# Loading the sorting network from SyncE ahead of q, dropping three trial instructions, and a newly searched instruction order in a fused attention and feed-forward kernel

## The chip, the cores and the metric

The kernel runs on one core of a Trainium2 chip. A core has TensorE (PE in the profile), VectorE (DVE), ScalarE (ACT), GpSimd (POOL) and SyncE (SP), each with its own stream of instructions, and 16 DMA engines that all of its transfers share. The metric is the device time of one execution in microseconds (us). A comparison gives the median of several runs.

## What is computed

Input are q, k, v of shape (4 batches, 8 heads, 768 positions, 64 channels), a sorting network `sort_net` of one 8x8 matrix for each of the 32 heads, and the two weights of a feed-forward part, `w_in` (512x2048) and `w_out` (2048x512), all float32.

```python
P = sort_net
for _ in range(5):
    P = exp(P - max(P, axis=-1))
    P = P / (sum(P, axis=-1) + 1e-09)
    P = P / (sum(P, axis=-2) + 1e-09)
k_sorted = einsum('bhij,bhjcd->bhicd', P, k in 8 blocks of 96 positions)
v_sorted = einsum('bhij,bhjcd->bhicd', P, v in 8 blocks of 96 positions)
attn = softmax(q_block @ k_sorted_block.T / 8)      # 96x96, block by block
x = (attn @ v_sorted_block), heads side by side      # 3072 rows x 512
out = relu(x @ w_in) ** 2 @ w_out                    # 3072 x 512
```

So five rounds of exponentials and row and column sums on the small matrices (Sinkhorn) come before everything else: no block of k or v can be mixed before they are done.

## The kernel before, in words

**Stages.** Work on TensorE goes in this order. First a start: `p_sb` (the 32 small matrices) is loaded, five Sinkhorn rounds alternate between ScalarE (the exponential, L465) and VectorE (sums, reciprocals and products, `sink_norm`, L409 to L413); meanwhile TensorE runs filler matmuls on a tile of ones (`fill`, L438) and transposes q of batch 0 (L578). Then `p_spread` (L489) brings P into the form from which the mixing weights `w_all` are built. Then comes batch 0, first halves, by a hand-written list, `FIRST`. Each entry is a letter for a step and a digit for the pair of heads: K and V mix k and v with P (L628), S makes scores (L699), T transposes v (L748), A multiplies by the values (L890), X transposes the result into `xT` (L943), F begins a feed-forward product (L970). An upper-case letter has its result copied out of PSUM by ScalarE, a lower-case one by VectorE; a prime, together with the kind of the step, says which of two pools of PSUM tiles it takes.

**The rest** is one stream of matmuls. The feed-forward part is cut into eight units of 384 rows: 64 matmuls "up" (L1012, four for each of 16 column tiles), a Relu on ScalarE (L1020), a square on VectorE (L1023), and three tiles of 16 matmuls "down" (L1042; the last tile of all is L1070). Steps of the attention of the batches to come are put between them: `s_sort2` (L664) mixes the second halves of batch 0, `s_nat` (L784) mixes k or v of the later batches, S and A as above. For v of batches 1 to 3 the mixed tile `vn` is written to DRAM (`v_way`, L808) and read back in another layout (`vblk`, L814) for A; k, q and most results are turned by DMA transposes (L839, L866, L925). All of these transfers and the outputs (L991) are issued by SyncE, in one queue, in one order.

**Loads.** SyncE first issues float32 q of heads 0 to 3 of batch 0 into spare space of `xT` (`q32`, two transfers, L270), and ScalarE casts them to bf16 (L473). ScalarE itself issues one transfer, that of `p_sb` (L265). GpSimd issues all other loads (L324): q of heads 4 to 7, k and v of batch 0, `w_in` and `w_out` in four parts each, then v, k and q of batch 1, and later batches 2 and 3 when a small copy has seen that a batch is done (L1159).

**Who decides the order.** `Plan` is a list scheduler that runs while the kernel is built. Every step is given an engine, a cost and its dependencies, and so is every transfer, as an operation on a pretended engine "DMA" or "WAY" with an assumed duration. TensorE has two lists, attention and feed-forward, each kept in its own order; an attention step goes ahead of a feed-forward step when it is ready and its due number is not above the count of feed-forward steps already placed. The due numbers are the table `DUES`, by batch and step: N and V are `s_nat` of k and v, Z the DMA transposes, L the loads of a batch, Q the first steps of batch 1, W the weights `w_t` that `s_nat` uses. The emitted instructions carry no times, only this order and the waits on data. Where the plan leaves TensorE idle before the feed-forward part, it puts in filler matmuls that last as long as the planned gap.

**Trial instructions.** Beside the real work there are three that compute nothing that is used: two float32 matmuls (L448) in `warm`, one exponential with an accumulated sum (L452) behind the first Sinkhorn exponential, and one reciprocal from PSUM (L456) in the third round. They have a VectorE memset (L443) as their input.

Of the kernel before, what the change touches and what calls it, by code (L numbers as in the profile page):

```python
# [8 lines left out]
FP32 = mybir.dt.float32  # L9
BF16 = mybir.dt.bfloat16  # L10
AF = mybir.ActivationFunctionType
# [10 lines left out]
    (0, "K"): (-242.5, -237.0, -449.5, -391.0),  # L22
    (0, "S"): (-214.5, -217.0, -359.5, -370.5),
    (0, "T"): (-167.5, -226.5, -373.0, -268.5),
    (0, "A"): (-159.0, -195.0, -306.0, -99.0),
    (0, "X"): (-124.0, -130.5, -290.5, -94.5),
    (0, "W"): (-245.5,),
    (1, "V"): (-115.0, -110.5),
    (1, "Q"): (-94.0,),
    (1, "N"): (None, -50.5),  # L30
    (1, "Z"): (None, None, 33.5, 34.0),
    (1, "S"): (-53.0, -3.0, 38.5, 51.0),
    (1, "A"): (-45.5, 3.5, 45.5, 51.0),
    (1, "X"): (43.5, 24.5, 56.0, 53.5),
    (2, "L"): (60.0,),
    (2, "N"): (66.5, 69.5),
    (2, "V"): (63.5, 79.5),
    (2, "Z"): (77.5, 81.5, 85.5, 81.5),
    (2, "S"): (80.0, 84.0, 102.5, 97.0),
    (2, "A"): (82.0, 86.0, 102.5, 98.0),  # L40
    (2, "X"): (90.5, 118.0, 111.0, 114.0),
    (3, "L"): (123.0,),
    (3, "N"): (132.0, 141.0),
    (3, "V"): (128.0, 138.5),
    (3, "Z"): (133.5, 133.5, 149.5, 143.0),
    (3, "S"): (147.0, 153.0, 161.0, 158.0),
    (3, "A"): (147.0, 154.5, 162.0, 158.5),
    (3, "X"): (156.5, 161.5, 195.0, 182.0),
# [4 lines left out]
FIRST = ("K0' v0 K1 v1 S0 t0' S1 t1' A0 K2' V2 A1 K3 S2 t2' v3' S3 x1' A2 T3' x0 A3 X2' F1 F0 "  # L53
         "F4 F3 F7 F6 X3")
# [130 lines left out]
def kernel(  # L185
# [10 lines left out]
    nc = tc.nc  # L196

    B, H, S, D = q.shape
# [31 lines left out]
    plan = Plan()  # L230
# [34 lines left out]
    nc.scalar.dma_start(out=p_sb, in_=sort_net.rearrange("b h i j -> (b h) i j"))  # L265
# [53 lines left out]
    landed = {}  # L319

    def dma(key, mb, dst_src, deps=(), long=True, rate=0.23):
        def issue(e):
            dst, src = dst_src()
            nc.gpsimd.dma_start(out=dst, in_=src)  # L324
        op = plan.add("POOL", 0.75, issue, deps)
        landed[key] = plan.add("DMA", mb / (0.39 if key[0] == 0 else 0.43 if long else rate), lambda e: None, [op, landed.get("last")])
        landed["last"] = landed[key]
# [25 lines left out]
    first = plan.add("DMA", 3.95, lambda e: None)  # L353
# [88 lines left out]
    t32 = xT[:, 3, 2 * S:].bitcast(FP32)  # L442
    nc.vector.memset(t32[:, 0:136], 1.0)  # L443

    def warm(e):
        fill(2.4, 0)
        for n in range(2):
            nc.tensor.matmul(out=p2[1][:, 0, 8 * n:8 * n + 8], lhsT=t32[:, 0:128],  # L448
                             rhs=t32[:, 128:136], start=True, stop=True)

    def try_exp(e):
        nc.scalar.activation(out=t32[:, 144:152], in_=t32[:, 128:136], func=AF.Exp,  # L452
                             accum_out=t32[:, 152:153])

    def try_rec(e):
        nc.vector.reciprocal(out=t32[:, 160:168], in_=p2[1][:, 0, 8:16])  # L456
# [7 lines left out]
    for it in range(5):  # L464
# [3 lines left out]
        if it == 0:  # L468
            plan.add("ACT", 0.3, try_exp, [step])
        if it < 2:  # L470
            def cast(e, g=it):
                alloc_qkv(0)
                nc.scalar.copy(out=qkv[0][0][:, 2 * g:2 * g + 2, :], in_=q32[g])  # L473

            casts.append(plan.add("ACT", 0.83, cast, [step, plan.add(
                "WAY", 3.5 + 0.9 * it, lambda e: None, tail=3.5 + 0.9 * it)]))
# [4 lines left out]
        if it == 2:  # L481
            plan.add("DVE", 0.0, try_rec, [step])
# [737 lines left out]
```

## Time and profile before

| | us |
|---|---|
| three runs | 218.44, 219.02, 220.64 (median 219.02) |
| the profiled execution's own time | 218.59 |
| its span, first to last instruction of the program | 216.8 |
| TensorE busy | 209.8 |
| ScalarE, VectorE busy | 121.4, 109.9 |
| GpSimd busy | 28.4 |
| mean granted TensorE clock | 0.998 of full speed |

A profile line of a group gives the line of the kernel, the engine, the operation, the tile written and the tiles read; `x16` is the number of instructions. "idle before, releaser" is how long the engine had nothing to run ahead of these and what ended it. The chain that ended last is followed back from the last instruction. Since matmuls are pipelined and their ends are modelled, the distance from the start of one group to the start of the next is the better measure of what a group costs on TensorE: 4 matmuls up are 0.65 us, 4 down 0.865 us, 16 of `s_nat` 0.31 us, 16 of S 0.45 us, 8 of A 0.25 us.

### The profile page before, as it was taken

To read this page: it belongs to the slowest core of one execution; us is meant where nothing else is said; L and a number is where in the kernel's file an instruction comes from. 1 tells how busy PE (TensorE), PEld (TensorE's weight loads), DVE (VectorE), ACT (ScalarE), POOL (GpSimd) and SP (SyncE) were. 2 spreads that over 40 slices of the span, in tenths; PEclk is the share of its full clock that TensorE was granted. 3 is DMA by queue.
4 is the path that set the end of the run, shared out by engine and by line. 5 is a ranking of instruction groups with operands and counts; after the bars stand their busy time and mean duration, and the time that the engine had idled before them with its cause. 6 is when DMAs were issued, how large, how long until landed. Compare 5 with 4: busy or idle time off the path is not lost.

```text
span 216.8 us, 5097 instructions
## 1 busy us (share of the span) xinstructions
PE 209.8 (97%) x2040; PEld 116.1 (54%) x2040; DVE 109.9 (51%) x300; ACT 121.4 (56%) x252; POOL 28.4 (13%) x53
## 2 busy tenths in 40 slices
PE   8898999799999999999999999999999999999994
PEld 3466765346655555445665455445655565456542
DVE  4778576345894447643895045517675154015300
ACT  5777985227783268436774177328865375147421
POOL 7994320000000700000000330000000000000000
PEclk9999999999999999999999999999999999999999
DMA  6999999999968799939852599599884310120012
GB/s 183 194 204 207 206 208 209 194 173 292 225 125 76 136 211 228 188 102 194 187 153 64 121 192 215 105 208 229 98 209 115 91 48 3 48 97 0 0 51 97
DMA packets 47864, 31.92 MB, mean 147 GB/s; under 512 B 27296, under 2 KB 42912, under 8 KB 47840
## 3 DMA queue, kind: packets, MB, share of 16 engines
q1 hardware_dynamic: 35568, 18.34, 37.8%
q0 software_dynamic: 12224, 13.24, 37.8%
q8 instruction: 16, 0.26, 0.5%
q14 instruction: 8, 0.07, 0.1%
q10 hardware_dynamic: 48, 0.01, 0.0%
HBM read 29.70 MB, written 8.72 MB: 177 GB/s over the span
## 4 chain that ended last, share of the span: by engine, by line
PE 81%; DMA 14%; POOL 3%; issue 1%; ACT 0%; POOLq 0%
PE op L1042 36%; PE hp L1012 34%; DMA vb<-in_v_dram 9%; DMA w_in_bf<-in_moe_w_in_dram 5%; PE p L890 3%; PE p L699 3%; PE p L784 2%; PE op L1070 2%; POOL vb L324 1%; POOL kb L324 1%; POOL qb L324 1%; PE qtp L578 0%; PE p L628 0%; PE xtp L943 0%; POOL ident masks.py:199 0%
## 5 line engine op out<-in xcount | busy, mean ns | idle before, releaser
L1012 PE MATMUL hp<-xT,w_in_bf 128*128 128x384 bf16 x506 | 88.1, 326 | 0.0
L1042 PE MATMUL op<-w_out_bf,h 128*128 128x512 bf16 x368 | 84.6, 379 | 0.0
L1020 ACT ACTIVATE h<-hp 128x384 bf16<-128x384 f32 x128 | 61.7, 495 | 17.8 <-PE hp L1012 14.7
L1023 DVE TENSOR_TENSOR h<-h 128x384 bf16<-128x384 bf16 x128 | 43.6, 354 | 44.2 <-ACT h L1020 43.8
L1012 PEld LDWEIGHTS <-w_in_bf 128*128 128x128 bf16 x506 | 47.3, 98 | 31.2 <-issue 0.7
L1042 PEld LDWEIGHTS <-h 128*128 128x128 bf16 x368 | 33.9, 98 | 38.3 <-issue 1.2
L248 ACT COPY ob<-op 128x512 f32<-128x512 f32 (+2 forms) x23 | 13.1, 568 | 48.7 <-PE op L1042 46.3
L728 ACT ACTIVATE et<-p 96x384 bf16<-96x384 f32 x48 | 19.7, 488 | 9.3 <-PE p L699 9.3
L901 DVE TENSOR_TENSOR ao<-p,rec 96x512 bf16<-96x512 f32 x32 | 22.0, 686 | 1.3 <-DVE rec L900 0.2
L890 PEld LDWEIGHTS <-et 96*128 96x128 bf16 x256 | 11.7, 97 | 5.2 <-issue 0.7
L250 DVE CAST vn<-p 128x768 bf16<-128x768 f32 x6 | 5.7, 958 | 15.1 <-PE p L784 10.7
L900 DVE RECIPROCAL rec<-p 96x8 f32<-96x8 f32 x32 | 6.4, 201 | 10.3 <-PE p L890 8.7
L1159 POOL COPY held<-xT 1x3 bf16<-1x3 bf16 (+1 forms) x2 | 0.4, 186 | 85.8 <-DMA xT<-ao 85.8
L248 ACT CAST vn<-p 128x768 bf16<-128x768 f32 x6 | 4.8, 800 | 9.1 <-PE p L784 9.1
L890 PE MATMUL p<-vblk,et 96*128 96x65 bf16 x192 | 9.6, 193 | 0.0
L438 PE MATMUL p<-ones 128*128 128x512 bf16 (+1 forms) x28 | 8.5, 433 | 1.1 <-DVE ones L274 1.1
L699 PEld LDWEIGHTS <-kvT 64*128 64x128 bf16 x256 | 6.2, 94 | 5.4 <-issue 3.1
L844 DVE COPY kvT<-kx 128x768 bf16<-128x768 bf16 x10 | 8.4, 847 | 0.0
L250 DVE CAST kn<-p 128x768 bf16<-128x768 f32 x5 | 4.8, 956 | 5.5 <-PE p L784 5.5
L324 POOL DMA_DIRECT2D kb<-in_k_dram x10 | 6.5, 646 | 4.1 <-DMA w_out_bf<-in_moe_w_out_dram 1.8
L324 POOL DMA_DIRECT2D vb<-in_v_dram x10 | 6.3, 630 | 3.0 <-DMA w_in_bf<-in_moe_w_in_dram 3.0
L324 POOL DMA_DIRECT2D qb<-in_q_dram x8 | 6.0, 750 | 2.7 <-DMA w_in_bf<-in_moe_w_in_dram 1.9
(88 smaller groups left out, 120.0 us busy)
## 6 DMA issues: line engine op xcount, KB each, us to landing
out_dram<-ob SPq DMA_DIRECT2D x23, 256.0 KB, 3.2
v_way<-vn SPq DMA_DIRECT2D x6, 396.0 KB, 5.3
vblk<-v_way SPq DMA_DIRECT2D x6, 396.0 KB, 4.1
vb<-in_v_dram POOLq DMA_DIRECT2D x6, 384.0 KB, 11.9
kb<-in_k_dram POOLq DMA_DIRECT2D x6, 384.0 KB, 10.4
qb<-in_q_dram POOLq DMA_DIRECT2D x6, 384.0 KB, 13.4
w_in_bf<-in_moe_w_in_dram POOLq DMA_DIRECT2D x4, 512.0 KB, 11.1
w_out_bf<-in_moe_w_out_dram POOLq DMA_DIRECT2D x4, 512.0 KB, 16.3
```

Source lines behind the costliest of these rows:

```text
L248: nc.scalar.copy(out=out, in_=in_)
L250: nc.vector.tensor_copy(out=out, in_=in_)
L324: nc.gpsimd.dma_start(out=dst, in_=src)
L438: nc.tensor.matmul(out=p2[slot][:, 0, 0:128 * r].rearrange("p (r x) -> p r x", r=r), lhsT=ones, rhs=ones[:, None, :].to_broadcast([128, r, ...
L699: nc.tensor.matmul(out=scp[:, h, BLK * n:BLK * (n + 1)], lhsT=u.ksT[64 * h:64 * (h + 1), HS * hf + BLK * n:HS * hf + BLK * n + 128], rhs=( ...
L728: nc.scalar.activation(out=et[:, h, 0:HS].rearrange("p (n c a) -> p n c a", c=C0, a=NA), in_=st["p"][0:96, h, 0:HS].rearrange("p (n a c) - ...
L890: nc.tensor.matmul(out=oup[:, h, 66 * n:66 * n + D + 1], lhsT=et_r[u.et[hf]][:, h, BLK * n:BLK * n + 128], rhs=(u.vs[:, NQ * hf + n, h, 0: ...
L901: nc.vector.tensor_tensor(out=u.ao[:, n0:n0 + NQ, :, :].rearrange("p n e d -> p e n d"), in0=ov[:, :, :, 0:D], in1=rec[:, :, :, None].to_b ...
L1012: nc.tensor.matmul(out=t["hp", nt][:, 0:HS], lhsT=w_in_bf[:, kc, 128 * nt:128 * (nt + 1)], rhs=xT[:, kc, t0:t0 + HS], start=(kc == 0), sto ...
L1020: nc.scalar.activation(out=t["h1", nt], in_=t["hp", nt][:, 0:HS], func=AF.Relu)
L1023: nc.vector.tensor_tensor(out=t["h2"][:, nt, :], in0=t["h1", nt], in1=t["h1", nt], op=ALU.mult)
L1042: nc.tensor.matmul(out=t["op", mt], lhsT=t["h2"][:, nt, 128 * mt:128 * (mt + 1)], rhs=w_out_bf[:, nt, :], start=(nt == 0), stop=(nt == NT ...
```

## The change

The load of `p_sb` is issued by SyncE as its first transfer, so that ScalarE issues none and the two transfers of `q32` come behind it in SyncE's queue. The casts of `q32` on ScalarE move from behind the first and second exponential to behind the second and third. The three trial instructions and their memset are gone. In the plan, loads of batch 0 are given a higher rate and every load a lag after its transfer, and the first landing moves from 3.95 to 4.15. With these assumptions `DUES` and `FIRST` are replaced.

```diff
-    (0, "K"): (-242.5, -237.0, -449.5, -391.0),
+    (0, "K"): (-265.0, -237.0, -495.0, -419.0),
...
-    (1, "V"): (-115.0, -110.5),
-    (1, "Q"): (-94.0,),
+    (1, "V"): (-117.0, -62.5),
+    (1, "Q"): (-58.5,),
...
-    (1, "S"): (-53.0, -3.0, 38.5, 51.0),
+    (1, "S"): (-45.5, -5.0, 5.0, 50.0),
...
-FIRST = ("K0' v0 K1 v1 S0 t0' S1 t1' A0 K2' V2 A1 K3 S2 t2' v3' S3 x1' A2 T3' x0 A3 X2' F1 F0 "
-         "F4 F3 F7 F6 X3")
+FIRST = ("K0' v0 K1 v1 S0 t0' S1 t1' A0 K2' V2 A1 K3 S2 t2 v3 S3 x1' A2 T3' x0' A3 X2' F0 F1 F3 "
+         "F4 F6 F7 X3")
...
-    nc.scalar.dma_start(out=p_sb, in_=sort_net.rearrange("b h i j -> (b h) i j"))
+    nc.sync.dma_start(out=p_sb, in_=sort_net.rearrange("b h i j -> (b h) i j"))
...
-        landed[key] = plan.add("DMA", mb / (0.39 if key[0] == 0 else 0.43 if long else rate), lambda e: None, [op, landed.get("last")])
-        landed["last"] = landed[key]
+        landed["last"] = plan.add("DMA", mb / (0.43 if key[0] == 0 or long else rate), lambda e: None, [op, landed.get("last")])
+        lag = ((0.4 if key[1] == 0 else 1.7 if key[1:3] == (2, H - 2) else 0.9) if key[0] == 0
+               else 0.05 if key[0] in (2, 3) else 1.9)
+        landed[key] = plan.add("DMA", lag, lambda e: None, [landed["last"]], tail=lag)
...
-    first = plan.add("DMA", 3.95, lambda e: None)
+    first = plan.add("DMA", 4.15, lambda e: None)
...
-    t32 = xT[:, 3, 2 * S:].bitcast(FP32)
-    nc.vector.memset(t32[:, 0:136], 1.0)
-
     def warm(e):
         fill(2.4, 0)
-        for n in range(2):
-            nc.tensor.matmul(out=p2[1][:, 0, 8 * n:8 * n + 8], lhsT=t32[:, 0:128],
-                             rhs=t32[:, 128:136], start=True, stop=True)
-
-    def try_exp(e):
-        nc.scalar.activation(out=t32[:, 144:152], in_=t32[:, 128:136], func=AF.Exp,
-                             accum_out=t32[:, 152:153])
-
-    def try_rec(e):
-        nc.vector.reciprocal(out=t32[:, 160:168], in_=p2[1][:, 0, 8:16])
...
-        if it == 0:
-            plan.add("ACT", 0.3, try_exp, [step])
-        if it < 2:
-            def cast(e, g=it):
+        if it in (1, 2):
+            def cast(e, g=it - 1):
...
-                "WAY", 3.5 + 0.9 * it, lambda e: None, tail=3.5 + 0.9 * it)]))
+                "WAY", (4.3, 5.8)[it - 1], lambda e: None, tail=(4.3, 5.8)[it - 1])]))
...
-        if it == 2:
-            plan.add("DVE", 0.0, try_rec, [step])
```

The instruction streams that this gives differ as follows. **TensorE, start:** the two trial matmuls are gone; behind the ten first filler matmuls stand 12 transposes of q, 6 fillers, 36 transposes, 4 fillers, and from there the same run as before (12 transposes and 1, 1, 3 and 2 fillers between, then `p_spread`); there are 28 fillers in both. **TensorE, batch 0:** the groups of `FIRST` stand in the same order, only the pools differ and the F pieces are exchanged in pairs. **TensorE, unit 0:** ahead of the first `s_nat` of batch 1's v stand 28 matmuls down instead of 8, with the same 64 up, mixes, S and A ahead of them; between the first and the second `s_nat` of v stand 12 matmuls down, an A and a transpose (20 matmuls down before). **TensorE, later:** 8 matmuls up now stand ahead of the transposes of q of batch 1; the first A that reads `vblk` stands behind 36 matmuls up instead of 28; some S groups of 16 are split into two of 8 or joined, and single `s_nat` groups of batches 2 and 3 change places. **SyncE:** one output transfer goes ahead of the first `v_way` write (none before), one stands between the first and the second as before, and one behind the second instead of two; of the later transfers some change places by one or two. **GpSimd:** the same instructions in the same order.

More of the change, by code (lines that the diff above doesn't have):

```diff
@@ L21 @@
 DUES = {
-    (0, "K"): (-242.5, -237.0, -449.5, -391.0),
[L23 to L27, printed above, removed]
-    (1, "V"): (-115.0, -110.5),
-    (1, "Q"): (-94.0,),
-    (1, "N"): (None, -50.5),
-    (1, "Z"): (None, None, 33.5, 34.0),
-    (1, "S"): (-53.0, -3.0, 38.5, 51.0),
[L33 to L48, printed above, removed]
-}
-FIRST = ("K0' v0 K1 v1 S0 t0' S1 t1' A0 K2' V2 A1 K3 S2 t2' v3' S3 x1' A2 T3' x0 A3 X2' F1 F0 "
-         "F4 F3 F7 F6 X3")
+    (0, "K"): (-265.0, -237.0, -495.0, -419.0),
+    (0, "S"): (-232.5, -234.0, -349.0, -310.0),
+    (0, "T"): (-184.0, -236.0, -400.0, -291.5),
+    (0, "A"): (-135.0, -150.0, -300.0, -111.0),
+    (0, "X"): (-58.0, -109.0, -251.5, -80.5),
+    (0, "W"): (-267.0,),
+    (1, "V"): (-117.0, -62.5),
+    (1, "Q"): (-58.5,),
+    (1, "N"): (None, -31.0),
+    (1, "Z"): (None, None, 2.5, 48.5),
+    (1, "S"): (-45.5, -5.0, 5.0, 50.0),
+    (1, "A"): (-27.0, -4.5, 31.5, 51.5),
+    (1, "X"): (40.0, 23.5, 37.0, 53.5),
+    (2, "L"): (40.0,),
+    (2, "N"): (75.5, 79.0),
+    (2, "V"): (60.5, 82.5),
+    (2, "Z"): (81.0, 82.5, 94.0, 83.5),
+    (2, "S"): (86.0, 86.5, 96.0, 93.5),
+    (2, "A"): (86.0, 88.0, 99.0, 94.5),
+    (2, "X"): (97.5, 103.0, 103.0, 102.0),
+    (3, "L"): (109.0,),
+    (3, "N"): (111.5, 130.0),
+    (3, "V"): (112.5, 144.0),
+    (3, "Z"): (128.5, 139.0, 153.0, 149.0),
+    (3, "S"): (144.0, 153.0, 158.0, 153.5),
+    (3, "A"): (145.0, 153.5, 159.5, 154.5),
+    (3, "X"): (150.5, 170.0, 236.5, 211.5),
+}
+FIRST = ("K0' v0 K1 v1 S0 t0' S1 t1' A0 K2' V2 A1 K3 S2 t2 v3 S3 x1' A2 T3' x0' A3 X2' F0 F1 F3 "
+         "F4 F6 F7 X3")
 class Op:
```

## The prediction

> **What bounds the kernel now.** I read the page's busy times first, then its chain, then TensorE's waits, then the chain in order of time, and last ScalarE's and TensorE's timelines of the first 13 us.
>
> ```profile
> PE 209.8 (97%) x2040; PEld 116.1 (54%) x2040; DVE 109.9 (51%) x300; ACT 121.4 (56%) x252; POOL 28.4 (13%) x53
> ...
> PE 81%; DMA 14%; POOL 3%; issue 1%; ACT 0%; POOLq 0%
> ```
>
> TensorE is busy 97% of the span, and the chain is TensorE but for some DMA. So only two things can move the end: when the stream of matmuls starts, and where it stands still. TensorE's waits name the latter:
>
> ```profile
> PE p L784 <- DMA vb<-in_v_dram: 1.4, 1, 1.4
> PE p L438 <- DVE ones L274: 1.1, 1, 1.1
> PE qtp L578 <- ACT qb L473: 0.6, 1, 0.6
> PE p L890 <- ACT qz L248: 0.5, 1, 0.5
> ```
>
> One wait is in the steady part: `s_nat` waits 1.4 us for v of batch 1. The chain says when:
>
> ```profile
> 18.89 20.09 DMA vb<-in_v_dram
> 38.98 0.04 issue
> 39.03 0.39 PE p L784 x16
> 39.41 4.42 PE op L1042 x20
> ```
>
> v lands at 38.98, and 20 matmuls down stand right behind the step that waits for it. From 39.03 to 213.65 the chain is TensorE alone. Now the start, ScalarE's timeline and then TensorE's:
>
> ```profile
> 0.74 0.44 ACTq L265 DMA_DIRECT2D p_sb<-in_sort_net_dram  x1
> 1.21 1.28 ACT L465 ACT_TABLE_LOAD   x1 [1.21 <-PEq L1204]
> 2.98 0.26 ACT L465 ACTIVATE p_sb<-p_sb 32x64 f32<-32x64 f32 x1 [0.49 <-DMA p_sb<-in_sort_net_dram]
> 4.08 0.83 ACT L473 CAST qb<-xT 128x768 bf16<-128x768 f32 x1 [0.65 <-DMA xT<-in_q_dram]
> 4.81 0.25 ACT L465 ACTIVATE p_sb<-p_sb 32x64 f32<-32x64 f32 x1
> 5.32 0.83 ACT L473 CAST qb<-xT 128x768 bf16<-128x768 f32 x1 [0.25 <-DMA xT<-in_q_dram]
> ```
>
> ```profile
> 6.20 0.56 PE L578 MATMUL qtp<-ident,qb 64*64 64x64 bf16 x24 [0.63 <-ACT qb L473]
> 6.70 0.82 PE L438 MATMUL p<-ones 128*128 128x512 bf16 x3
> ...
> 12.21 0.47 PE L489 MATMUL pt_ps<-p_ij,xT 32*128 32x32 bf16 x8
> ```
>
> The first exponential waits for `p_sb`. Exponentials start at 2.98, 4.81, 6.57, 8.33 and 10.09, so 1.76 a round, 1.83 in the first, where a cast stands in the way. `p_spread` at 12.21 has two paths of nearly the same length: the rounds (VectorE has what it reads first at 12.05), and TensorE's own run of transposes and fillers, without a gap from 6.20, when the second cast is done.
>
> **The change, part by part.**
>
> *v of batch 1 (a wait goes).* 64 matmuls up and the same mixes, S and A stand ahead in both; instead of 8 matmuls down there are 28. Twenty at 0.216 us are 4.3 us more work, so TensorE asks for v at 37.63 + 4.3 = 41.9 instead of 37.63, and v is there since 38.98 with 2.9 to spare (2.5 if the stream starts 0.4 earlier). The 1.39 us go. What could be late instead is `w_out`: the fourth part was issued at 17.41 and took 19.5 to land, 36.9; the first 12 matmuls down need 2.6 us from 35.7, so it is asked for at 38.3, or 37.9 with the earlier start: 1.0 spare. Gain **1.39**.
>
> *p_sb on SyncE.* Nothing in the trace shows an 8 KB load as SyncE's first. From above it takes the 2.2 of the same load on ScalarE's queue (landing 2.96); from below the 1.6 of the 64 KB output (2.34). The exponential also needs the table load, which ran 1.21 to 2.49 behind ScalarE's own issue and allowed an exponential at 2.98 at the latest, 1.77 after its start; without the issue it starts 0.44 earlier, so at the latest the exponential can run at 2.54. In the trace this load shares the engines with q's, issued at the same 0.74; in front of q in one queue it need not. I take 2.55, and 2.98 as the other end.
>
> *q behind it, casts later.* One issue (0.47) delays q's landings from 4.05 and 5.29 to 4.52 and 5.76. With 1.76 a round the exponentials come at 2.55, 4.30, 6.06, 7.82, 9.58. The first cast runs at 4.55 to 5.38, behind it the `sel` copy to 5.9, before the third exponential. The second runs behind that, 6.24 to 7.07. TensorE's run behind it, by rows of before: 36 transposes 0.81, four fillers 0.95, four groups of 12 transposes 1.24, fillers of 1, 1, 3 and 2 pieces 0.42, 0.75 and 0.54: 4.71. `p_spread` then starts at 7.12 + 4.71 = 11.83; the rounds are done at 9.58 + 1.96 = 11.54. So fillers now set it, and a faster `p_sb` is not paid in full: 12.21 - 11.83 = 0.38. With the exponential at 2.98 the second cast ends at 7.48 and `p_spread` starts at 12.24. Ends: a gain of 0.4, a loss of 0.03; I take **0.38**. GpSimd's weight builds (13.36, when its loads are issued) and the landings of k and v for the last pair (15.37 and 16.09, read at 16.52 and 17.62) leave at least 0.6 spare.
>
> A rule against this: the Trainium skill, "DMA: Bandwidth & Descriptors", Issuing engines are not separate DMA queues, says that transfers interleave whichever engine started them, and that a second issuing engine saves only issue time. By that p_sb gains nothing and q loses its 0.47. The 2.2 us for 8 KB beside q agree that they interleave; that being ahead in one queue gains nothing, no row shows. By the rule the end result is 0.4 later than mine. And "ScalarE: Activation LUTs", What ACT_TABLE_LOAD costs, gives 1283 ns and a drain of 1380 ns behind it; the row has 1.28 and an exponential 0.49 after its end, so at most 0.49 of drain here. With the page's sum the exponential could not start before 3.43, 0.45 later than in the trace of before.
>
> *Trial instructions.* TensorE's two took 0.44 us before a wait for the first cast anyway; ScalarE's ran in the 1.1 us in which VectorE had the matrices, VectorE's in the 0.2 that ended with an exponential. Cost and gain 0; bounds 0 and 0.07, the first round's excess, which is in the start above.
>
> *The order behind.* Laid end to end from the second halves of batch 0 (21.51) with the rows of before (4 up 0.65, 4 down 0.865, and 0.10 more when S, `s_nat` or transposes follow; S 0.28 for 8 and 0.45 for 16; A 0.25; `s_nat` 0.31), the groups sum to 190.17 before and 190.29 after: **0.12** lost to more changes between kinds. In the trace the same stretch takes 2.0 more than 190.17: 1.39 for v, and about 0.6 in small waits, each under 0.3.
>
> *SyncE and v's way back.* v_way's first write now stands behind an output, and its source is mixed at 41.7 instead of 39.03, so it is issued at about 43.1 (40.58 before). Its landing took 11.9, to 52.5, while GpSimd's loads filled the engines until 52.48 (last q issued 31.47, 21.0); the second, issued 4.7 later, took 9.6 and landed 2.4 behind. Both are then paced by the end of those loads and not by their issue. I expect 53 to 54 and, as `vblk` took 5.0, 58 to 59 for the first. The first A that reads it stands at 59.17 in the laid-out order, 0.38 earlier by the start, 0.2 later by a wait at `s_nat` of k as in the trace (0.50 where the others are 0.31): 59.0. Bounds: none, and 1.0 if all 11.9 and 5.0 are paid from 43.1 (60.0). I take 0.
>
> *Tighter turns.* In places S, exponential and A now follow at 1.39 us (S at 62.3, A at 63.7), where the row needs 0.28 for S, 0.86 for two exponentials and hand-overs, about 1.4. I add **0.2** for two or three such.
>
> *Later loads.* Batch 2's loads start when the third `xT` transpose of batch 1 lands; its last A stands at 66.6 in the layout, 66.68 in the trace. Nothing moves. The other `s_nat` steps find data landed 4 us and more before. At the end the last transpose landed 0.2 before the matmuls that need it (168.82 + 2.9 against 171.9); the distance from its A is the same 20 matmuls down, so it stays just covered.
>
> **Sum**, against the profiled execution's own 218.59 (the median of the runs, 219.02, is 0.43 above): -1.39 - 0.38 + 0.12 + 0.2 = -1.45, **217.1**.
>
> **Rivals.**
> *A, the start gains nothing:* `p_sb` lands at 2.96 again, or q later still. For it: 16 engines serve both transfers, and TensorE's run behind the second cast is fixed. Against: nothing is ahead of it now. -1.39 + 0.03 + 0.12 + 0.2: 217.5.
> *B, slower: v's way back replaces the wait for v.* The write stands behind a 256 KB output that is behind transposes which landed at 46.1. If the queue is paced by the loads, the 396 KB took 46.1 to 52.5, 6.4; an output ahead takes 256/396 of that, 4.1, so it would land at 56.6, the return at 61.6, and A at 59.0 waits 2.6: 217.1 + 2.6 = 219.7. Against: the loads end at 52.5, after which the trace drains three outputs and a write in 3.1 us. It decides when `vblk` lands after 60.5, when the wait passes the 1.45 gained. Half of it (the 1.0 above) gives 218.1.
> *C, the wait only moves:* `w_out`'s fourth part or v lands later since q's load is behind. It needs 1.0 for `w_out`; the delay is 0.47 and the bytes are the same. -0.38 + 0.12 + 0.2: 218.5.
> *D, the small waits fall too:* the order meets its data and the 0.6 go to 0.1, without my 0.2: 217.1 - 0.7 = 216.4.
>
> **How the numbers follow.** Forecast 0.42 (own range 216.7 to 217.5), A 0.20, the half of B 0.11, B 0.09, C 0.05, D 0.13. One per cent, about what a measurement of this kernel tells from no change, is 2.2 us: faster means below 216.8 against the median. That is D, and a third of the forecast's cases (the start gains more, or fewer turns are tight): 0.27. Slower by 1% (above 221.2) would need B beyond its price or several waits; 0.10 with the chance that the later order has a wait that I do not see. The rest, 0.63, is within 1%. The range leaves out the best of D and the worse of B: 216.0 to 219.2.
>
> **What would show it.** Right: the first exponential near 2.55, `p_spread` near 11.8, no wait of `s_nat` for `vb`, `vblk` landed before 59, and from the second halves of batch 0 to the end about 0.7 above 190.29. Wrong: a wait of A for `vblk` or of the matmuls down for `w_out`; `p_spread` at 12.2 or later; waits of PE for exponentials or for VectorE's products between 60 and 67 above 0.5 in all.

## The result and the profile after

The changed kernel takes 218.12 us in the median (217.63 to 218.66, 18 runs), the kernel before 218.83 beside it (218.32 to 220.64, 18 runs): ratio 0.9962, interval 0.9947 to 0.9976. So it is faster: by 0.71 us in the medians, by about 0.8 by the ratio. The forecast was 217.1, a gain of 1.45. The profiled executions have spans of 216.8 before and 216.2 after, a gain of 0.6.

The changed kernel's page, busy times and chain:

```profile
PE 209.8 (97%) x2020; PEld 115.9 (54%) x2036; DVE 109.2 (51%) x297; ACT 122.1 (56%) x251; POOL 28.3 (13%) x53
...
PE 93%; DVE 2%; ACT 2%; issue 1%; DVEq 0%
```

TensorE's busy time is what it was, and DMA (14% of the chain before) is gone from the chain. TensorE's waits in the changed kernel (what waited, for what, us in total, times, longest):

```profile
PE p L440 <- DVE ones L274: 1.1, 1, 1.1
PE p L875 <- ACT qz L248: 0.5, 1, 0.5
PE p L684 <- DVE ao L886: 0.3, 1, 0.3
PE op L1027 <- issue: 0.2, 1, 0.2
```

The line with `vb` is gone, and a wait of 0.3 for `ao` is new. The chain in order of time (start, us) shows the place where `s_nat` had waited:

```profile
36.04 5.78 PE op L1027 x26
41.82 0.31 PE p L769 x16
42.13 0.97 PE op L1027 x4
```

`s_nat` starts at 41.75 by TensorE's timeline (the chain counts from the modelled end of the matmul before it); v landed at 39.30, and `w_out`'s last part at 37.24. No wait is left here, as forecast. ScalarE's first work:

```profile
2.50 0.26 ACT L454 ACTIVATE p_sb<-p_sb 32x64 f32<-32x64 f32 x1 [0.48 <-DMA p_sb<-in_sort_net_dram]
...
4.42 0.81 ACT L460 CAST qb<-xT 128x768 bf16<-128x768 f32 x1
...
6.02 0.26 ACT L454 ACTIVATE p_sb<-p_sb 32x64 f32<-32x64 f32 x1 [0.27 <-DVE p_sb L415]
6.48 0.83 ACT L460 CAST qb<-xT 128x768 bf16<-128x768 f32 x1 [0.20 <-DMA xT<-in_q_dram]
```

The first exponential is at 2.50 (forecast 2.55), but the second cast waits for q, which landed at 6.45 and not at 5.76. `p_spread` still starts at 11.88 (forecast 11.83, before 12.21): the cast ends 0.24 later than forecast, and `p_spread` follows its end by 4.57 instead of the forecast's 4.76. Two more things differ. From `p_spread` to the second halves of batch 0 it is 9.49 instead of 9.30 us. And from there to the end TensorE's starts fall 1.20 behind the groups laid end to end, where the prediction expected about 0.7. (It counted to the end of the last matmul, which gave 2.0 for the kernel before; by starts that is 1.79, so that on this measure some 0.5 was to be expected.)

My theory for the lost half, ahead of the experiments: the start is worth less than in this profile, since q is late; VectorE stands still once in batch 0; v's way back is late in batch 2; and short waits in tight turns have grown. The main rival: the gain was lost in the start alone.

### The profile page after: what moved, and what is told of

It reads as the page before. It is cut to its first block, busy times and chain, and to the rows that moved or that the text cites. A ratio compares the mean times of both kernels' runs of the same rounds, so it can differ in the third digit from the quotient of the medians.

```text
span 216.2 us, 5062 instructions
## 1 busy us (share of the span) xinstructions
PE 209.8 (97%) x2020; PEld 115.9 (54%) x2036; DVE 109.2 (51%) x297; ACT 122.1 (56%) x251; POOL 28.3 (13%) x53
## 4 chain that ended last, share of the span: by engine, by line
PE 93%; DVE 2%; ACT 2%; issue 1%; DVEq 0%
PE hp L997 37%; PE op L1027 36%; PE p L875 4%; PE p L440 4%; PE p L684 3%; PE p L769 2%; PE op L1055 2%; PE qtp L563 2%; DVE ao L886 1%; PE vbp L733 1%; PE p L649 1%; DVE h L1008 1%; ACT h L1005 1%; PE xtp L928 1%; PE hp L955 0%
## 5 line engine op out<-in xcount | busy, mean ns | idle before, releaser
L1027 PE MATMUL op<-w_out_bf,h 128*128 128x512 bf16 x352 | 83.3, 379 | 0.9 <-issue 0.2
L248 ACT COPY ob<-op 128x512 f32<-128x512 f32 (+2 forms) x25 | 14.2, 568 | 49.1 <-PE op L1027 46.6
L875 PEld LDWEIGHTS <-et 96*128 96x128 bf16 x256 | 11.2, 97 | 5.5 <-issue 0.7
L440 PE MATMUL p<-ones 128*128 128x512 bf16 (+1 forms) x28 | 9.2, 460 | 1.1 <-DVE ones L274 1.1
L248 ACT CAST kn<-p 128x768 bf16<-128x768 f32 x5 | 4.0, 806 | 4.7 <-PE p L769 4.7
```

The costliest lines, as they stand in the source:

```text
L248: nc.scalar.copy(out=out, in_=in_)
L440: nc.tensor.matmul(out=p2[slot][:, 0, 0:128 * r].rearrange("p (r x) -> p r x", r=r), lhsT=ones, rhs=ones[:, None, :].to_broadcast([128, r, ...
L875: nc.tensor.matmul(out=oup[:, h, 66 * n:66 * n + D + 1], lhsT=et_r[u.et[hf]][:, h, BLK * n:BLK * n + 128], rhs=(u.vs[:, NQ * hf + n, h, 0: ...
L1027: nc.tensor.matmul(out=t["op", mt], lhsT=t["h2"][:, nt, 128 * mt:128 * (mt + 1)], rhs=w_out_bf[:, nt, :], start=(nt == 0), stop=(nt == NT ...
```

## Experiments

Sixteen runs, in five groups. Times are medians; "ratio" is against the kernel before, run beside it on the same chip, with its interval; the runs were spread over four chips. Where profiles are compared, the numbers of the start are in the table behind group 3.

### 1. Start and order apart

**Network on ScalarE again** (changed kernel):

```diff
-    nc.sync.dma_start(out=p_sb, in_=sort_net.rearrange("b h i j -> (b h) i j"))
+    nc.scalar.dma_start(out=p_sb, in_=sort_net.rearrange("b h i j -> (b h) i j"))
```

> The changed kernel with one line put back: the sorting network is loaded by ScalarE again, q is SyncE's first load; casts, trial instructions and order stay changed. Theory (being ahead of q in one queue is what makes the network's load land early): it lands near 2.96 again instead of 2.48, the first exponential starts near 2.98, the exponentials follow every 1.76 without a cast between the first two, the second cast stands behind the third (6.50 + 0.26) and ends near 7.6, so the products that spread P start near 12.3 instead of 11.88, and the kernel takes 0.3 to 0.45 more than the changed one. Rival (the gain at the start comes from the casts' places and from the trial instructions that are gone, the load's place is worth nothing): the products start at 11.9 or before, because q lands 0.47 earlier, and the time is that of the changed kernel or 0.1 to 0.4 less.

218.03, ratio 0.9942 (0.9913 to 0.9970): not slower than the changed kernel's 0.9962. The mechanism went as the theory had it. ScalarE's timeline of this run:

```profile
6.52 0.26 ACT L454 ACTIVATE p_sb<-p_sb 32x64 f32<-32x64 f32 x1 [0.27 <-DVE p_sb L415]
6.68 0.81 ACT L460 CAST qb<-xT 128x768 bf16<-128x768 f32 x1
```

The network landed at 2.97, q at 3.96 and 5.22, and the second cast waits only for the third exponential. `p_spread` starts at 12.19, 0.31 behind the changed kernel's profile. But the time does not show the 0.31 (it would make the ratio 0.9976, above this interval), so the changed kernel's 11.88 is probably not what most of its executions have.

**Old tables in the changed kernel, new tables in the old one** (`DUES` and `FIRST` exchanged, all else as it was):

> The changed kernel with the due times and the list of first steps of the kernel before: only the start is changed. Theory (v of batch 1 lands by the stream of loads, at 39.0 to 39.3, whatever TensorE does): s_nat waits for v again, about 1.5 to 1.8 us, since it asks for it earlier by what the start gains; the gain of the start is eaten by that wait, and the time is within 0.15 of the kernel before, ratio 0.9995 to 1.0007. Rival (the gains of the start and of the order add up): the wait stays 1.4 and the time falls by what the spreading products gain, 0.33: ratio 0.9985.

220.09, ratio 1.0037 (1.0012 to 1.0063). Neither theory: the lags in the plan stayed, and with them the old tables give a third order. It has 28 matmuls down ahead of v's `s_nat`, as the changed kernel has, and no wait for v, but new waits elsewhere (0.5 for the transposed `ao`).

> The kernel before with the due times and the list of first steps of the changed kernel: only the order is changed; trial instructions and the network's load by ScalarE stay. Theory (the order is worth 1.46 for v less 0.12 for changes of kind, 0.33 for the new wait of A for v's copy in batch 2 and about 0.5 of short waits in tight turns; the start brought 0.14 from the second halves on): 0.5 to 0.6 less than the kernel before, about 0.1 to 0.15 more than the changed one, ratio 0.9974, and A waits for v's copy at about 112.5 here too. Rival (the lost gain lies at the start, where something new holds TensorE in the changed kernel): with the old start the order brings its full 1.2, ratio 0.9945, and the time is below that of the changed kernel.

222.63, ratio 1.0157 (1.0123 to 1.0191). Also another order, with 8 matmuls down ahead of v's `s_nat`, which waits 1.6 for v by TensorE's waits.

Both fell as tests of start against order. They show something else: what takes v's wait away are the plan's corrected assumptions on landings (rate and lags) and not the due times. Without them the new tables ask for v behind 8 matmuls; with them, even the old tables put 28 in front.

**Order alone** (kernel before, with tables, lags and the first landing of the changed kernel):

```diff
-        landed[key] = plan.add("DMA", mb / (0.39 if key[0] == 0 else 0.43 if long else rate), lambda e: None, [op, landed.get("last")])
-        landed["last"] = landed[key]
+        landed["last"] = plan.add("DMA", mb / (0.43 if key[0] == 0 or long else rate), lambda e: None, [op, landed.get("last")])
...
-    first = plan.add("DMA", 3.95, lambda e: None)
+    first = plan.add("DMA", 4.15, lambda e: None)
```

> The kernel before with the due times, the list of first steps, the landing lags and the 4.15 of the changed kernel; the network on ScalarE, the early casts and the trial instructions stay. From the second halves of batch 0 on, every engine has the changed kernel's order (the earlier run with new tables but without the lags had another order and says nothing of this one). Theory (the move of the network brings the first exponential forward by 0.5 and q's second load back by 1.2 to 1.8, so that the start gains nothing on the whole): the products that spread P start at 12.2, the second halves at 21.5, and the time is within 0.15 of the changed kernel, ratio 0.996 to 0.997. Rival (the start is worth the 0.38 of the prediction): 0.38 slower than the changed kernel, ratio about 0.998.

218.48, ratio 0.9974 (0.9948 to 1.0000). Seven of its 12 runs lie at 217.89 to 218.49, where the changed kernel lies, and five at 219.56 to 221.26. The profiled one is of the five (219.56): TensorE ran at half pace until 9.9 us, so that `p_spread` started at 13.90 and nothing behind it is early. TensorE there, three fillers:

```profile
7.19 1.46 PE L440 MATMUL p<-ones 128*128 128x512 bf16 x3
```

The same three took 0.82 in the kernel before. No wait for v is left. So in the seven lower runs the order alone brings what the whole change brings. This order with the old start also has VectorE's stop (group 3) at the cheaper place, 9.30 in the table there against 9.49 to 9.51, so equal times leave up to 0.2 for the changed kernel's start; the runs do not tell 0.15 from 0.38.

**The changed kernel again**, on the chip of three others:

> The changed kernel unchanged, on the chip of the three runs beside it, so that they can be compared with it there. What is asked: where q's second load lands. In the trace of the changed kernel it landed at 6.45, in two runs of kernels with the same first loads at 7.09 and 7.13, and with the network on ScalarE at 5.22 to 5.33; the prediction had 5.76. Theory (behind the network, q's second load is issued after GpSimd's first load and shares the engines with it, which makes it late by a varying amount): it lands between 6.3 and 7.2, and the ratio is 0.9962 as before, within 0.0015. Rival (the 7.1 belong to the edits of those two kernels): 6.45 again, within 0.1.

218.42, ratio 0.9961 (0.9946 to 0.9976), as at first. ScalarE:

```profile
7.03 0.83 ACT L460 CAST qb<-xT 128x768 bf16<-128x768 f32 x1 [0.83 <-DMA xT<-in_q_dram]
```

q landed at 7.00, and `p_spread` starts at 12.40: in this execution the start loses 0.19 against the kernel before's profile, where in the first it gained 0.33. So the theory holds: q's landing varies, and it is late without any edit.

### 2. Why q is late

**One memset, then three, on GpSimd ahead of its first load:**

```diff
+    late = const.tile([128, 384], FP32, name="late")
+    for n in range(3):
+        nc.gpsimd.memset(late, 0.0)
     load(0, 0, HP, HP, slice(0, 64))
```

> The changed kernel with one memset of 128x384 on GpSimd ahead of its first load, which nothing reads; GpSimd's two loads of q for the other pairs are issued some 0.3 to 0.6 later, about when or after SyncE issues q's second load at 1.67. Theory (q's second load is late because GpSimd's load of q goes ahead of it): it lands near 5.8 instead of 6.45 to 7.1, the second cast starts right behind the third exponential, near 6.25, and the products that spread P start near 11.85 every time; against the changed kernel's runs the median falls by 0.1 to 0.4. Rival (the engines serve both in any case, or the second load is late because it stands third in SyncE's queue): it lands at 6.4 or later still, and the time is that of the changed kernel.

218.04, ratio 0.9951 (0.9934 to 0.9969). This tests nothing: the one memset ran before GpSimd could issue, and the load went at 1.28 instead of 1.25. q landed at 6.39.

> The changed kernel with three memsets of 128x384 on GpSimd ahead of its first load (one alone was over before that load could be issued: it went at 1.28 instead of 1.25, so that run tested nothing). GpSimd's first load of q now goes near 1.7 to 1.8, with or after q's second load on SyncE at 1.67. Theory (GpSimd's load of q, issued first, keeps the engines from q's second load): that load lands at 5.6 to 6.0 instead of 6.4 to 7.0, the second cast starts near 6.25, and the products that spread P start at 11.7 to 11.9 instead of 11.8 to 12.5; the median falls by 0.1 to 0.4 against the changed kernel. Rival (the network's load in front of it in SyncE's queue is what delays it): it lands at 6.4 or later with GpSimd's loads out of the way, and the time stays or rises.

218.29, ratio 0.9950 (0.9926 to 0.9973). GpSimd's first load now goes at 2.05, and SyncE's second load of q lands at 6.15, earlier than in any other run with the network ahead of it, but not at 5.6 to 6.0. So GpSimd's load is part of the delay at most, and one profile of a landing that varies by 1.4 us does not show even that; the cause stays open. The time gains nothing, since GpSimd's q is late in turn (8.14) and the transposes wait 0.6 for it by TensorE's waits.

### 3. VectorE's stop in batch 0

Of VectorE's timelines, first the kernel before, then the changed one (in each the second line is the instruction that starts late, among the reciprocals and products of the first two A steps):

```profile
15.83 0.20 DVE L900 RECIPROCAL rec<-p 96x8 f32<-96x8 f32 x1
16.27 0.69 DVE L901 TENSOR_TENSOR ao<-p,rec 96x512 bf16<-96x512 f32 x1 [0.23 <-DVE rec L900]
```

```profile
15.73 0.69 DVE L886 TENSOR_TENSOR ao<-p,rec 96x512 bf16<-96x512 f32 x1
16.76 0.20 DVE L885 RECIPROCAL rec<-p 96x8 f32<-96x8 f32 x1 [0.34 <-ACT kvT L248]
```

Elsewhere a product follows its reciprocal by 0.24; before, it took 0.44. In the changed kernel the reciprocal's wait is over at 16.31, and it starts 0.45 later. The copies to `kvT` that the bracket names do not explain it: with one memset (below) they end at the same distances from `p_spread`, and the reciprocal starts 0.40 sooner. In both traces the late instruction is the 64th that VectorE's record holds, waits on semaphores counted.

**Nine, one, two and three small memsets on VectorE**, which nothing reads (n is 9, 1, 2 or 3):

```diff
+    pad = const.tile([32, 16], FP32, name="pad")
+    for n in range(9):
+        nc.vector.memset(pad[:, n:n + 1], 0.0)
+
     def warm(e):
```

> The changed kernel with nine very small memsets on VectorE before the first round; nothing reads them. In the changed kernel the second reciprocal of batch 0 starts 0.34 late although its products are there, and it is VectorE's 64th instruction in the profile; in the kernel before the 64th is the product of the first A, and it is that which starts 0.23 late. Theory (VectorE stands still for some 0.4 us at a fixed place of its stream, by the count of instructions): the stop moves onto the second block of the weights at 12.87, where VectorE idles 0.33 anyway; the second reciprocal starts near 16.4 instead of 16.76, the second halves of batch 0 start near 21.2 instead of 21.37, and the time falls by 0.1 to 0.25, ratio to the kernel before near 0.995. Rival (the delay belongs to that instruction: a wait that the profile does not name): the reciprocal stays at 16.7 to 16.8 and the time within 0.05 of the changed kernel.

217.47, ratio 0.9931 (0.9900 to 0.9961). The stop is gone from sight: the reciprocal starts 0.62 behind the product, without idle time. The absolute times of the expectation were missed, since q landed at 7.09 here; the distance from `p_spread` to the second halves is 9.12 instead of 9.49.

> The changed kernel with one small memset on VectorE before the first round, which nothing reads. Theory (VectorE stops at a fixed count of its instructions): the stop moves by one instruction, from the second reciprocal of batch 0 to the product in front of it, as in the kernel before; that product starts about 0.2 to 0.25 later than 0.24 after its reciprocal, and the time is within 0.15 of the changed kernel. Rival (the delay is that reciprocal's own): the reciprocal starts 0.34 late again and the product in front of it on time.

217.58, ratio 0.9926 (0.9902 to 0.9950). No late instruction at all; distance 9.12. I had not counted the semaphore wait between product and reciprocal: with one memset the 64th is that wait, which VectorE takes while the product of 0.69 still runs.

```profile
15.78 0.69 DVE L890 TENSOR_TENSOR ao<-p,rec 96x512 bf16<-96x512 f32 x1
16.40 0.20 DVE L889 RECIPROCAL rec<-p 96x8 f32<-96x8 f32 x1
```

> The changed kernel with two small memsets on VectorE before the first round. The run with one showed no stop at all, so a stop at a fixed count, moved by one, is not what it is. Two theories are left. A: the stop depends on where the stream is cut into pieces that are an even number of instructions long, and shows only where an instruction is asked for at once; then two memsets bring it back, on the product of the first A, as in the kernel before, whose stream is two instructions longer too: that product starts 0.2 to 0.25 late. B: any shift takes it away, and the kernel before has its stop for a reason of its own: no delay on VectorE between 15 and 18.

One execution, 218.83. The 64th is the product of the first A, and it starts 0.44 behind its reciprocal, as in the kernel before; distance 9.30, as there.

```profile
16.84 0.20 DVE L889 RECIPROCAL rec<-p 96x8 f32<-96x8 f32 x1
17.28 0.69 DVE L890 TENSOR_TENSOR ao<-p,rec 96x512 bf16<-96x512 f32 x1 [0.24 <-DVE rec L889]
```

> The same with three memsets. Theory A (pieces of an even number): no delay, as with one and with nine. Theory C (a fixed count, but the stop with one memset was hidden by chance): a delay on the first reciprocal of batch 0 (the instruction in front of that product), 0.2 to 0.35.

One execution, 221.09 (q landed at 7.70; TensorE's clock fell, which the last section shows). The 64th is the first reciprocal, 0.45 behind a semaphore wait that was over:

```profile
19.33 0.20 DVE L889 RECIPROCAL rec<-p 96x8 f32<-96x8 f32 x1 [0.46 <-PE tp L617]
```

So the count it is, and my theory of even pieces falls: here the 64th instruction did not start until some 0.45 us after the one ahead of it. What the stop is, the profile does not say. The table has every profile; by what the 64th is (a reciprocal, a product, or one that costs nothing), the distance takes three values to within 0.02, and another only where the clock fell.

| run | network landed | q's second load landed | `p_spread` | second halves | distance |
|---|---|---|---|---|---|
| before | 2.96 | 5.29 | 12.21 | 21.51 | 9.30 |
| order alone (network on ScalarE) | 2.93 | 5.08 | 13.90 | 23.20 | 9.30 |
| network on ScalarE | 2.97 | 5.22 | 12.19 | 21.70 | 9.51 |
| changed | 2.48 | 6.45 | 11.88 | 21.37 | 9.49 |
| changed, again | 2.40 | 7.00 | 12.40 | 21.91 | 9.51 |
| GpSimd, one memset | 2.43 | 6.39 | 11.79 | 21.30 | 9.51 |
| GpSimd, three | 2.52 | 6.15 | 12.49 | 22.00 | 9.51 |
| v read early | 2.36 | 6.40 | 11.80 | 21.30 | 9.50 |
| an A moved | 2.43 | 6.89 | 12.29 | 21.80 | 9.51 |
| VectorE, nine memsets | 2.37 | 7.09 | 12.49 | 21.61 | 9.12 |
| v read early, nine memsets | 2.47 | 6.58 | 11.98 | 21.10 | 9.12 |
| VectorE, one | 2.39 | 6.52 | 11.92 | 21.04 | 9.12 |
| VectorE, two | 2.38 | 7.82 | 13.22 | 22.52 | 9.30 |
| VectorE, three | 2.35 | 7.70 | 14.83 | 24.81 | 9.98 |
| old tables | 2.32 | 7.13 | 12.54 | 22.04 | 9.50 |
| new tables (network on ScalarE) | 3.00 | 5.33 | 12.24 | 21.54 | 9.30 |
| four edits (group 5, nine memsets) | 2.27 | 6.73 | 11.63 | 20.76 | 9.13 |
| the same, network on ScalarE | 2.85 | 7.62 | 12.49 | 21.62 | 9.13 |

### 4. Later waits: v's copy in batch 2, and a tight turn

**v's second half of batch 2 read back one step earlier** in SyncE's queue (the plan's list of steps, one moved):

```diff
-    for op in plan.run():
+    ops = list(plan.run())
+    ops.insert(612, ops.pop(621))
+    for op in ops:
```

TensorE in the changed kernel, the S that feeds the first A of that half, and the A:

```profile
110.96 0.34 PE L684 MATMUL p<-qz,kvT 64*128 64x96 bf16 x8
...
112.43 0.41 PE L875 MATMUL p<-vblk,et 96*128 96x65 bf16 x8
```

A starts 1.47 behind S. The chain names the exponentials as what it waited for, since they end last; but `vblk` landed at 112.29, 0.14 ahead.

> The changed kernel with one step moved in SyncE's queue: the reading back of v's second half of batch 2 stands ahead of the transpose of q that was right in front of it. Nothing else moves. Theory (the 0.33 that the first A of that half waits at 112.4 come from the reading's place in SyncE's queue): it is issued near 104.7 instead of 106.04 and lands before 111, the wait of A for vblk is gone, and the time falls by 0.2 to 0.35 against the changed kernel on this chip, with the transposed q landing later by 0.5 but unread until long after. Rival (a queue of transfers paced by the engines and not by the issue, or a transpose that is now late): it lands near 112 all the same, or S waits in its place, and the time stays.

218.05, ratio 0.9953 (0.9936 to 0.9970), 0.37 below the changed kernel beside it (218.42), in ranges that overlap. The reading is issued at 104.63 and lands at 108.66:

```profile
110.89 0.34 PE L684 MATMUL p<-qz,kvT 64*128 64x96 bf16 x8
...
112.04 0.41 PE L875 MATMUL p<-vblk,et 96*128 96x65 bf16 x8
```

A now starts 1.15 behind S, with the exponentials where they were. So the wait was for `vblk`; it is no effect of the exponentials. But the other runs bound what it is worth. Of 11 profiles with this order and the late reading, three have the wait (0.33, 0.36 and 0.21, the A each time 0.14 behind the landing); in eight the same issue landed in time. With the early reading, none of four has it (landings at 107.9 to 108.7). It is a wait that some executions have.

**One A of batch 3 moved** behind the next four matmuls down (`ops.insert(930, ops.pop(927))`):

> The changed kernel with one A of batch 3, the second of two in a row at 161.8, moved behind the next four matmuls down; nothing else moves. Theory (the short waits in tight turns, 0.12 to 0.14 each at five places, are what the order costs beyond the forecast, and each goes when the step is asked for later): TensorE's starts behind it stand 0.12 lower against the laid-out order, and the time falls by about 0.1. Rival (the wait moves on to the transposes of the last batch, which were just covered): the wait of 0.12 comes back at the matmuls that need the last transposes, 171 to 172, and the time stays.

218.00, ratio 0.9951 (0.9933 to 0.9970). In the changed kernel two A steps stand together and take 0.62 to the next group, where two rows of 0.25 make 0.50:

```profile
161.81 0.78 PE L875 MATMUL p<-vblk,et 96*128 96x65 bf16 x16
162.43 1.67 PE L1027 MATMUL op<-w_out_bf,h 128*128 128x512 bf16 x7
```

```profile
161.92 0.41 PE L875 MATMUL p<-vblk,et 96*128 96x65 bf16 x8
162.18 1.03 PE L1027 MATMUL op<-w_out_bf,h 128*128 128x512 bf16 x4
163.04 0.41 PE L875 MATMUL p<-vblk,et 96*128 96x65 bf16 x8
```

Moved apart (second fence), the step of 0.12 is gone, and it does not come back at the last transposes: from the second halves to the end the starts fall 0.78 behind the layout instead of 0.87 to 0.89. For 0.1 us the ratio is too coarse; the trace carries it.

### 5. Together

**Early reading and nine memsets:**

> The changed kernel with the two edits that took a delay away alone: v's second half of batch 2 is read back one step earlier in SyncE's queue, and nine small memsets on VectorE move its stop near the 64th instruction to where it idles. Theory (both delays lie on TensorE's path one after the other, 0.36 and 0.37): they add up, the time is 0.6 to 0.8 below the changed kernel, ratio to the kernel before 0.992 to 0.9935. Rival (the stream is caught up behind the first, at data that land by the stream of loads): only one of them shows, 0.35, ratio 0.9945.

217.60, ratio 0.9932 (0.9911 to 0.9952). This lies in the range of the first theory, that the two add up, but the nine memsets alone give as much (0.9931): in the median the second edit adds nothing that the runs show, as is to be expected of a wait that three executions in eleven have.

**Four edits** (the two above, the A moved, and each piece of filling that the plan has behind 7.9 us made 0.25 us shorter, seven filler matmuls fewer in all; only the last is shown):

```diff
-                fill(op.gap - (0.5 if op in pes else 0.05), slot)
+                fill(op.gap - (0.5 if op in pes else 0.05) - (0.25 if op.begin > 7.9 else 0.0), slot)
```

> The changed kernel with four edits: v's second half of batch 2 read back one step earlier, nine small memsets on VectorE, the A of batch 3 moved behind four matmuls down, and TensorE's fillers behind the second cast each 0.25 us shorter (seven pieces fewer). The first three were worth 0.0 to 0.36, 0.37 and 0.11 each in traces. Theory (the start's gain is lost because q's second load lands at 6.4 to 7.0 and TensorE's own run of transposes and fillers of 4.7 us stands behind it): with fewer fillers the products that spread P start 0.2 to 0.6 earlier, at 11.6 to 11.9, where the rounds end; the time is 217.0 to 217.4, ratio 0.990 to 0.9925. Rival (fillers set nothing: the transposes wait for copies or data): the products start at 11.9 to 12.3, and the time is that of the three edits, ratio 0.9925 to 0.9935.

217.41, ratio 0.9917 (0.9883 to 0.9951); six of its 11 runs are at 216.84 to 217.41. TensorE's timeline around `p_spread`:

```profile
10.60 0.39 PE L440 MATMUL p<-ones 128*128 128x512 bf16 x1
11.63 0.52 PE L478 MATMUL pt_ps<-p_ij,xT 32*128 32x32 bf16 x6 [0.65 <-DVE p_ij L426]
```

Though q landed at 6.73, `p_spread` starts at 11.63: it now waits 0.65 for VectorE's rounds, and no longer for fillers. This is the lowest median of all. Its interval lies below 1 and meets that of the changed kernel (0.9947 to 0.9976) only at its edge; what the fewer fillers add to the other edits (0.9932 without them and the moved A) the times alone do not tell.

**The same with the network on ScalarE:**

> The run beside it with the network loaded by ScalarE again, q first on SyncE. Theory (ahead of q the network starts the rounds 0.5 earlier, but delays q's second load by 1.2 to 1.8, and the fillers were what turned that into a loss): here the rounds set the products, at 12.0 to 12.1, and the time is 0.1 to 0.4 above the run beside it. Rival (the network's place is worth nothing either way): within 0.1 of it.

217.95, ratio 0.9931 (0.9900 to 0.9963), 0.54 above the run beside it (the best five are at 217.23 to 217.94 against 216.84 to 217.02). The rounds set `p_spread` as the theory had it, but at 12.49 and not at 12.0 to 12.1: the first exponential is 0.57 later than in the run beside it, and q's second load landed at 7.62, so that the second cast (7.64 to 8.47) stood in the way of the fourth exponential. Nothing was ahead of q in SyncE's queue here, and four other profiles with the network on ScalarE have 5.1 to 5.3: the place alone does not settle that landing. The network's place is worth something as soon as TensorE's own run no longer sets `p_spread`; how much, two overlapping intervals do not say; the traces have 0.57 at the first exponential.

## Why the prediction was half wrong

The main step, that v's wait goes, came as forecast. The steps that failed are terms of the sum. "Tighter turns" was put at 0.2 and measured 0.54. "SyncE and v's way back" was put at 0 and measured 0.33, in a batch that was not looked at. "Trial instructions: cost and gain 0" left out VectorE's stop, 0.19. And the gain at the start, put at 0.38, held for the profiled execution (0.33) but not for most others.

The account of the two profiled executions, term by term; "measured" comes from the steps of TensorE's starts against the groups laid end to end:

| term | forecast | measured |
|---|---|---|
| v of batch 1 | -1.39 | -1.46 |
| start, to `p_spread` | -0.38 | -0.33 |
| VectorE's stop | not in it | +0.19 |
| order, changes of kind | +0.12 | +0.12 |
| v's way back | 0 | +0.33 |
| tighter turns | +0.20 | +0.54 |
| sum | -1.45 | -0.61 |

- **v of batch 1: right**, and so is that rival C did not happen: `w_out`'s last part was there 0.96 us and v 2.45 us before they were asked for.
- **"q behind it, casts later": wrong in size.** "One issue (0.47) delays q's landings from 4.05 and 5.29 to 4.52 and 5.76." The first landed at 4.34. The second landed at 6.39 to 7.82 in the 12 profiles with the network ahead of it and GpSimd's first load at 1.24 to 1.28: 0.6 to 2.1 later than forecast, 1.1 to 2.5 later than before. Then the step behind it, "fillers now set it", turned the delay into `p_spread`: 11.79 to 13.22 and once 14.83, in six of the eleven with all fillers later than the 12.21 of before. The forecast of 11.83 agreed with five of the eleven (11.79 to 11.98), the profile of the result among them, and the other six are 0.46 and more above it. So for about half of the executions rival A was right: their start gains nothing. The link is shown: in ten of the eleven `p_spread` came 4.54 to 4.57 behind the end of the second cast, wherever that was (in the eleventh the clock fell), and with seven fillers fewer 4.04. Why q's second load lands so late, and so differently, stays open.
- **"p_sb on SyncE": right**, 2.27 to 2.52 instead of 2.85 to 3.00. The Trainium skill, "DMA: Bandwidth & Descriptors", Issuing engines are not separate DMA queues, holds that a transfer gains nothing by the engine that issues it but the issue. Here the network was issued at 0.74 from either engine and landed about 0.5 earlier when q's issue stood behind it. That does not contradict the page, since q was also issued 0.47 later; no run here has the same issue times in two queues.
- **Missing: VectorE's stop.** A stop was in the trace of before, 0.23 at the product of the first A, and it went unread. Dropping two instructions of VectorE moved it onto a reciprocal, and it cost 0.37 instead of 0.18. "Trial instructions: cost and gain 0" was wrong by this.
- **"SyncE and v's way back": "I take 0" was right for batch 1** (`vblk` landed at 57.27, forecast 58 to 59; rival B did not happen) and never looked at batch 2. There the second v step, the last of four in both kernels, came at 95.80 instead of 94.75, the writing went at 97.82 instead of 96.29, and the reading, behind transposes, at 106.04 instead of 103.67. "Later loads" ("Nothing moves") was right of the loads themselves (v of batch 2 landed at 79.22 and 86.30, before at 78.98 and 86.56) and did not follow v any further.
- **"Tighter turns": the kind was right, the sum too small.** Behind v's step the starts fell 0.33 behind the layout before, and 0.87 now without the wait for `vblk`: 0.54 more and not 0.2. The steps are at 64.2 (0.13), 70.3 (0.05), 103.1 (0.14), 113.9 (0.13) and 162.4 (0.12), each within 0.02 in all profiles of this order. Only the last was undone by an edit; that the other four would go the same way is argued.

The medians differ by 0.71 and the profiled executions by 0.64 (218.59 and 217.95). The account closes for the profiles; for the medians, with q's landing different in each execution, only to some 0.3. Two things bear on this. With the changed kernel's order and the stop on the reciprocal, a profiled execution's own time less the start of its `p_spread` is 205.7 to 206.2 in seven profiles (and 205.4 to 205.5 in the five where the stop costs nothing). From these an estimate: the median of 218.12 stands for a `p_spread` between 11.9 and 12.4. And in the kernel before the chain runs through v's landing and not through the start: as long as v's wait is not used up, an execution that starts later waits less for v. So its usual `p_spread` cannot be read from its median, and 12.21 is that of one profile.

## What to carry to other kernels

A gain at the start is worth only what the next thing behind it lets through: when an issue is put in front of another, bound the later one's landing by more than the time of the issue, above all while other queues send, and look at what turns its delay into a wait (here fillers of fixed length). A forecast that agrees with one profile can agree by luck (11.83 against 11.88, with q 0.69 later than forecast, and half of the executions elsewhere); where a landing varies between executions, look at several. And after a reordering, follow each round trip through memory in every batch: the one that was studied was right, the one that was not looked at was late.

## What the runs showed of the hardware

- **VectorE's 64th instruction** (semaphore waits counted) did not start until 0.43 to 0.47 us after the start of the one ahead of it, in each profile in which it could be seen, a product or a reciprocal. It costs nothing where the engine is busy or idle anyway. One useless memset of 0.06 us took 0.37 out of batch 0 here.
- **TensorE's pace at the start varies** between executions of one program. The ten first fillers took 3.62 to 4.45 us. Fillers of 512 columns start 0.43 us apart up to the moment at which the trace's record of the granted clock begins, and 0.22 apart behind it; that moment lies between 3.70 and 9.90 us in the 18 profiles. The run with three memsets stood idle for 1.77 us before 8.61, and then the granted clock fell (the column before the last two):

```profile
8.00:10.00 2.00, 1.40 (x40) 0.95 (x40) 0.78 (x4) 2.00 (x6) 1.37 (x2) 1.00 1.31 201
...
12.00:14.00 2.00, 2.00 (x20) 0.81 (x17) 0.72 (x5) 0.51 (x2) 1.96 (x3) 0.50 1.34 208
```

At 0.50 the same matmuls took twice as long, and the kernel 221.09. The run with two memsets idled 1.69 at the same place and kept 1.00. The Trainium skill, "TensorE: Matmul & The Clock Gate", The HAM clock gate, tells of a window of 3.4 us that runs freely, so that the same program meets it at different points. The traces agree: but for the last one, which the end of the record cuts off, each stretch of one granted clock is a whole multiple of 3.413 us, 59 to 64 of them in most, and two at 1.00 (3.70 to 10.52) and two at 0.50 (10.52 to 17.35) in the run with three memsets. Laid out from the first stretch, this grid has 1.50 us of that run's pause in one piece, and parts the 1.69 of the other into 1.19 and 0.50. That fits one fall in two like pauses; where the limit lies, two pauses do not show.
- **A late `vblk` was named as the exponentials' fault.** The releaser in a chain is the wait that ended last by the record; a transfer that lands 0.14 ahead of the start can hide behind it. The distance from the step that feeds it, 1.47 against 1.15, told them apart.
